# Pooled attention and a ResMLP on one core: rearranging the preamble of batch 0 (constants, bias row, second kpT cast, last heads, lambda alpha1 of the rests)

## The chip, the cores and the metric

The kernel runs on one core of a Trainium2 chip. Times are device microseconds (us) of one execution. Every kernel was run several times, each time beside runs of the kernel before on the same chip; p1 to p3 below are single runs of the change, made for three more profiles.

The engines are called TensorE (PE in the profile; PEld are its weight loads), VectorE (DVE), ScalarE (ACT), GpSimd (POOL), and the queue that issues most loads (SP).

## The reference, cut to what matters

```python
# q, k, v: (8, 8, 576, 64); pool = 8
k_p = k.reshape(B, H, 72, 8, 64).mean(axis=3)
v_p = v.reshape(B, H, 72, 8, 64).mean(axis=3)
attn = softmax(q @ k_p^T / 8)
x = (attn @ v_p)                     # heads joined: (8, 576, 512)
# ResMLP
a1 = alpha1 * x + beta1
u = x + lam * (w_tok @ a1)           # mixes the 576 tokens
a2 = alpha2 * u + beta2
out = u + lam * (relu(a2 @ w_ch1) @ w_ch2)
```

## The kernel before: the parts that matter

The kernel folds lam and alpha1 into `lamal_bc`, keeps `xs = lam*alpha1*x` as the input of the token mixing, and brings in `lam*beta1` as a product of one **bias row** (row 64 of the last chunk of `xs`) with the row sums of w_tok. Each 576-token batch is four chunks of 128 tokens and a rest of 64. Of the helpers that are not shown, `att_F` transposes q, `att_K` spreads the pooled k into `kpT`, `att_S` makes the scores of one head (S) and ScalarE their exponentials (`ET`), `att_Vrem` places the pooled v of the rest, and `keep_warm` issues products that nobody reads, to keep TensorE busy.

```python
def row_of_xs(i, eng):                      # the bias row, 1 x 512
    p0 = 64 - 64 * i
    eng.tensor_tensor(out=xs_pool[i][p0:p0 + 1, 4, :], in0=vecs[p0:p0 + 1, 2],
                      in1=vecs[p0:p0 + 1, 0], op=ALU.mult)

def sum_v(b, u, eng=nc.vector):             # pools 4 heads of v: adds of 512, 256, then 128 columns
    t = st1[b]["v"][u]
    for n in (4, 2):
        eng.tensor_tensor(out=t[:, :, 0:n], in0=t[:, :, 0:n], in1=t[:, :, n:2 * n], op=ALU.add)
    ...

def att_V(b, u, copy):                      # one product spreads pooled v over partitions
    ps_v = gp("ps_v")
    nc.tensor.matmul(out=ps_v[:, 0:128], lhsT=sel_main..., rhs=st1[b]["v"][u]...)
    ...                                     # two casts into vp1
def att_AV(b, h): ...                       # 5 products of a head, then reciprocal and x on VectorE
def att_X(b, h0, h1, eng=nc.vector): ...    # xs = x * lamal, four chunks and the rest
def setup_wtok(tcx, copy): ...              # 5 transposes of w_tok, one evacuation
def setup_rowsum(tcx): ...                  # 5 products with ones, 128 columns each
def mix_T(b, c, eng=nc.vector): ...         # 5 products: one token chunk mixed; then u and u_bf
def mix_uT(key): ...                        # 4 transposes of u, needed by the channel MLP
```

The order in which the preamble of batch 0 issues these (the scheduling is by hand, each engine takes its own in this order):

```python
fill_E()                                    # 12 constants of ET, VectorE
sum_k(0, 0, nc.vector)
cast_rem(0, nc.gpsimd)
cast_q(0, 1, nc.gpsimd.tensor_copy)
row_of_xs(0, nc.vector)
...
load_wtok()                                 # issued by GpSimd
sum_v_rem(0, nc.gpsimd)                     # pools v's rest
for g in range(2):
    load_w1(g)                              # w_ch1, issued by GpSimd
att_S(0, 0); att_S(0, 1)
sum_k(0, 1, nc.vector)                      # the second half of k
att_F(0, 1); att_S(0, 2)
att_K(0, 1, nc.vector.tensor_copy)          # kpT: two casts
att_S(0, 3)
v_00 = st1[0]["v"][0]
sum_v(0, 0)                                 # first half of v, VectorE
att_Vrem(0, nc.scalar.copy)
nc.gpsimd.memset(v_00[:, 0, 0, 0:1], 0.0)   # makes GpSimd wait for VectorE's sum
sum_v(0, 1, nc.gpsimd)                      # second half of v, GpSimd
att_S(0, 4); att_S(0, 5)
att_V(0, 0, nc.vector.tensor_copy)          # "V1" below
att_AV(0, 0) ... att_AV(0, 3)               # with att_S(0, 6), att_S(0, 7), att_X
att_V(0, 1, nc.scalar.copy)                 # "V2" below
setup_wtok(0, nc.scalar.copy)
att_AV(0, 4)
...                                         # w_tok, heads 5 to 7 and row sums in turn
setup_vectors()
keep_warm(2)
mix_T(0, 0)
```

Three moments mark the path in what follows: the **landing of k** (start of VectorE's sum of the second half of k), **V2** (the product that spreads the second half of v, without which heads 4 to 7 cannot start) and **uT** (the first transposes of u).

The softmax here doesn't subtract the row's maximum and nothing guards it: scores larger than these inputs give would overflow.

Of the kernel before, what the change touches and what calls it, by code (L numbers as in the profile page):

```python
# [23 lines left out]
def kernel(  # L24
# [108 lines left out]
    def sum_k(b, u, eng):  # L133

        t = st1[b]["raw"][u][:, 1]
        bf = work.tile([P, 2, 2, D], BF, tag="k_bf", bufs=3, name="k_bf")
        for n in (4, 2):
            eng.tensor_tensor(out=t[:, :, 0:n], in0=t[:, :, 0:n], in1=t[:, :, n:2 * n], op=ALU.add)  # L138
        eng.tensor_tensor(out=bf, in0=t[:, :, 0:1].to_broadcast((P, 2, 2, D)),
                          in1=t[:, :, 1:2].to_broadcast((P, 2, 2, D)), op=ALU.add)  # L140
        st1[b]["k"][u] = bf
# [99 lines left out]
    def fill_E():  # L241
        for t in ET_pool:
            nc.vector.memset(t[:, 0:64], 1.0)
            nc.vector.memset(t[:, 64 + S:], 1.0)
# [25 lines left out]
    def row_of_xs(i, eng):  # L270
# [4 lines that stand above are left out]
# [87 lines left out]
    def att_F(b, u):  # L362



        st = st1[b]
        ps_q = gp("ps_q").bitcast(BF)
        for i in range(8):
            nc.tensor.transpose(  # L369
                out=ps_q[:, 128 * i:128 * i + 128],  # L370
                in_=st["q"][u][:, 2 * i:2 * i + 2].rearrange("p j d -> p (j d)"),
                identity=identity_bf)
        nc.scalar.copy(  # L373
            out=qT_of(b, u)[:, :, 0:256].rearrange("p h (x i) -> p h x i", i=4),
            in_=ps_q.rearrange("p (i a g h) -> p h (a g) i", i=4, a=2, h=4))
# [101 lines left out]
        nc.vector.tensor_tensor(out=x[:, :, dd:dd + D], in0=av[:, :, 0:64],  # L477
                                in1=rec.unsqueeze(2).to_broadcast((P, 5, D)), op=ALU.mult)

    def att_X(b, h0, h1, eng=nc.vector):  # L480

        x, xs = st1[b]["x"], xs_pool[b % 2]
        cols = slice(D * h0, D * h1)
        eng.tensor_tensor(  # L484
            out=xs[:, 0:4, cols], in0=x[:, 0:4, cols],
            in1=lamal_bc[:, cols].unsqueeze(1).to_broadcast((P, 4, D * (h1 - h0))), op=ALU.mult)
        p0 = 64 * (b % 2)
        eng.tensor_tensor(out=xs[p0:p0 + 64, 4, cols], in0=x[p0:p0 + 64, 4, cols],
                          in1=lamal_bc[p0:p0 + 64, cols], op=ALU.mult)
# [111 lines left out]
    nc.scalar.copy(out=lamal_bc, in_=ps_lamal)  # L601
    cast_q(0, 0, nc.vector.tensor_copy)
    att_F(0, 0)
    fill_E()
    sum_k(0, 0, nc.vector)
    cast_rem(0, nc.gpsimd)
    cast_q(0, 1, nc.gpsimd.tensor_copy)
    row_of_xs(0, nc.vector)
    att_Frem(0, (0,), nc.scalar.copy)
    att_K(0, 0, nc.vector.tensor_copy, nc.scalar.copy)  # L610
    att_Frem(0, (1,), nc.vector.tensor_copy)
    load_wtok()
    sum_v_rem(0, nc.gpsimd)
    for g in range(2):
        load_w1(g)
    att_S(0, 0)
# [1 line left out]
    sum_k(0, 1, nc.vector)  # L618
    att_F(0, 1)
    att_S(0, 2)  # L620
    att_K(0, 1, nc.vector.tensor_copy)
    att_S(0, 3)
    v_00 = st1[0]["v"][0]
    sum_v(0, 0)
    att_Vrem(0, nc.scalar.copy)
    nc.gpsimd.memset(v_00[:, 0, 0, 0:1], 0.0)
    sum_v(0, 1, nc.gpsimd)
    att_S(0, 4)
    att_S(0, 5)
    att_V(0, 0, nc.vector.tensor_copy)  # L630
    att_AV(0, 0)
# [7 lines left out]
    att_V(0, 1, nc.scalar.copy)  # L639
    setup_wtok(0, nc.scalar.copy)  # L640
    att_AV(0, 4)
    setup_wtok(1, nc.scalar.copy)
    att_AV(0, 5)
    load_qk(1, 0, nc.vector)
    load_rem(1)
    load_qk(1, 1)
    load_v_rem(1)
    load_v(1, 0)
    load_v(1, 1)
    att_X(0, 4, 6, nc.gpsimd)  # L650
    setup_wtok(2, nc.scalar.copy)
    att_AV(0, 6)
    setup_rowsum(0)
    setup_rowsum(1)
    setup_wtok(3, nc.scalar.copy)
    att_AV(0, 7)
    att_X(0, 6, 8)
    setup_rowsum(2)
    setup_rowsum(3)
    setup_vectors()  # L660
    keep_warm(2)
    mix_T(0, 0)
    mix_T(0, 1)
    mix_T(0, 2, nc.gpsimd)
    mix_uT((0, 0))
# [128 lines left out]
```

## Time and profile before

| | before |
|---|---|
| three runs | 368.33, 368.71, 368.93 us |
| the profiled run | 368.53 us (span 366.7) |
| landing of k, second half | 10.99 us |
| V2 | 19.27 us |
| first mixing of tokens | 25.51 us |
| first transposes of u (uT) | 28.75 us |

A line of the timeline gives start, length, engine, source line, operation, output and inputs by name, the shapes and the count of a merged group. At the end stand the idle time of the engine just before it and what ended that.

VectorE before, its sum of the first half of v in two lines:

```profile
14.96 1.15 DVE L416 TENSOR_TENSOR v_u<-v_u 128x512 f32<-128x512 f32 x2
16.15 0.29 DVE L418 TENSOR_TENSOR v_sum<-v_u 128x128 f16<-128x128 f32 x1
```

The reader is to see three things. GpSimd has issued w_ch1's loads by 15.15 and then stands idle 1.35 us, until VectorE's sum of v has ended at 16.44: VectorE releases it. GpSimd's own sum takes 2.06 us for its first two adds, and V2 starts 2.67 us after that sum began. And V2 has no idle time before it: there TensorE arrived at about the same time as the sum.

In this profile slow matmuls are not to be read from the row of granted clock (the share of TensorE's full clock that the profile lists): it shows full speed in the stretches where the row sum `ps_rs` took 0.62 us as in those where it took 0.39. The durations of like instructions show it.

### The profile page before, as it was taken

The numbers are of one execution on the slowest core, as the hardware profiler recorded it, in microseconds if no ns is written. First come the engines' busy times: TensorE is split into PE (matmuls) and PEld (weight loads), VectorE is DVE, ScalarE is ACT, GpSimd is POOL, SyncE is SP. The second block draws the span as 40 slices with busy tenths as digits, with TensorE's granted clock in tenths as the row PEclk, the third lists the DMA queues.
The fourth block names the chain that finished last, engine by engine and source line by source line (L and its number), as shares of the span: only waits on it lengthen the run. The fifth ranks groups of instructions, "written<-read, shape, count | busy, mean of one in ns | idle before, by whom it ended". The sixth has DMA issues, their size and how long they took to land.

```text
span 366.7 us, 6128 instructions
## 1 busy us (share of the span) xinstructions
PE 352.8 (96%) x2300; PEld 194.5 (53%) x2342; DVE 212.3 (58%) x433; ACT 215.8 (59%) x424; POOL 126.5 (34%) x182
## 2 busy tenths in 40 slices
PE   5799999999999999999999999999999999999995
PEld 2477555455545554555455554555455544544544
DVE  7765534883785368734864388627852687543011
ACT  3865994379628970698259923895279615712710
POOL 8866913072508141452346130905090500000000
PEclk9999999999999999999999999999999999999999
DMA  7999894039103901183108302480110002002002
GB/s 252 268 228 332 226 286 133 22 100 358 53 30 123 323 12 48 57 276 111 59 29 295 124 31 56 139 278 29 50 38 2 29 30 58 2 29 86 2 30 84
DMA packets 19575, 43.27 MB, mean 118 GB/s; under 512 B 2193, under 2 KB 4565, under 8 KB 19546
## 3 DMA queue, kind: packets, MB, share of 16 engines
q1 hardware_dynamic: 17488, 37.89, 30.2%
q0 software_dynamic: 1888, 4.86, 7.0%
q8 instruction: 18, 0.29, 0.3%
q10 hardware_dynamic: 170, 0.14, 0.2%
q14 instruction: 11, 0.09, 0.1%
HBM read 38.30 MB, written 9.44 MB: 130 GB/s over the span
## 4 chain that ended last, share of the span: by engine, by line
PE 87%; ACT 6%; DVE 3%; DMA 2%; issue 1%; SPq 1%; ACTq 0%
PE ps_ch L580 33%; PE ps_h L557 30%; PE ps_tok L510 9%; PE ps_sc L453 4%; ACT Hj L562 3%; PE ps_av L470 2%; PE ps_uT L541 2%; DMA qk_raw<-in_k_dram 2%; PE ps_q L369 1%; PE ps_tok L526 1%; ACT qT L373 1%; PE ps_w L288 1%; SPq L84 1%; PE ps_av L473 1%; PE ps_kp L401 1%
## 5 line engine op out<-in xcount | busy, mean ns | idle before, releaser
L557 PE MATMUL ps_h<-u_fm,w 128*128 128x512 bf16 (+1 forms) x574 | 133.4, 373 | 1.6 <-ACT u_fm L543 0.4
L580 PE MATMUL ps_ch<-w,Hj 128*128 128x512 bf16 x495 | 124.0, 379 | 1.2 <-issue 0.3
L562 ACT ACTIVATE Hj<-ps_h,bias_cols 128x512 bf16<-128x512 f32 x144 | 97.1, 691 | 33.9 <-PE ps_h L557 33.3
L557 PEld LDWEIGHTS <-w 128*128 128x128 bf16 x592 | 63.9, 114 | 48.6 <-issue 0.9
L580 PEld LDWEIGHTS <-Hj 128*128 128x128 bf16 x592 | 55.5, 98 | 49.4 <-issue 0.7
L543 ACT COPY u_fm<-ps_uT 128x512 bf16<-128x512 bf16 x36 | 21.1, 588 | 70.6 <-PE ps_uT L541 70.5
L484 POOL TENSOR_TENSOR xs<-x_tm,lamal_bc 128x512 bf16<-128x512 f32 x24 | 30.6, 1274 | 82.6 <-DVE x_tm L477 82.6
L455 ACT ACTIVATE ET<-ps_sc 128x288 f16<-128x288 f32 (+1 forms) x128 | 51.5, 488 | 11.5 <-PE ps_sc L453 11.1
L408 DVE CAST kpT<-ps_kp 64x288 bf16<-64x288 f32 x31 | 14.1, 455 | 44.0 <-PE ps_kp L404 43.8
L587 DVE TENSOR_TENSOR u_sb<-u_sb,ps_ch 128x512 f32<-128x512 f32 (+1 forms) x37 | 24.9, 673 | 24.9 <-PE ps_ch L580 21.0
L510 PE MATMUL ps_tok<-xs,wtT 128*128 128x512 bf16 (+1 forms) x155 | 38.7, 379 | 0.2
L586 DVE TENSOR_TENSOR ps_ch<-lam_bc,ps_ch 128x512 f32<-128x512 f32 x32 | 22.2, 693 | 25.5 <-PE ps_ch L580 25.4
L475 DVE RECIPROCAL rec<-ps_av 128x5 f32<-128x5 f32 x64 | 12.4, 193 | 36.8 <-PE ps_av L473 36.6
L477 DVE TENSOR_TENSOR x_tm<-ps_av,rec 128x320 f32<-128x320 f32 x64 | 31.5, 492 | 2.8
L138 POOL TENSOR_TENSOR qk_raw<-qk_raw 128x512 f32<-128x512 f32 (+1 forms) x28 | 30.2, 1078 | 1.1
L453 PE MATMUL ps_sc<-qT,kpT 128*128 128x288 bf16 (+1 forms) x128 | 29.4, 306 | 1.0 <-DVE kpT L408 0.8
L512 DVE TENSOR_TENSOR u_sb<-x_tm,ps_tok 128x512 f32<-128x512 f32 x32 | 21.9, 685 | 9.8 <-PE ps_tok L510 9.3
L685 POOL COPY ticks<-ticks 1x1 f32<-1x1 f32 x6 | 1.1, 178 | 70.5 <-DVE ticks L681 70.5
L510 PEld LDWEIGHTS <-wtT 128*128 128x128 bf16 (+1 forms) x160 | 15.0, 98 | 19.1 <-DVE xs L484 2.0
L470 PEld LDWEIGHTS <-ET 72*128 72x128 f16 (+1 forms) x256 | 17.1, 102 | 14.1 <-DVE vp L428 0.6
L513 DVE TENSOR_TENSOR u_bf<-u_sb,al_bc 128x512 bf16<-128x512 f32 x31 | 21.8, 704 | 1.1
L416 DVE TENSOR_TENSOR v_u<-v_u 128x512 f32<-128x512 f32 (+1 forms) x30 | 20.8, 693 | 0.8
(121 smaller groups left out, 338.9 us busy)
## 6 DMA issues: line engine op xcount, KB each, us to landing
qk_raw<-in_q_dram SPq DMA_DIRECT2D x16, 512.0 KB, 6.7
qk_raw<-in_k_dram SPq DMA_DIRECT2D x16, 512.0 KB, 6.5
v_u<-in_v_dram SPq DMA_DIRECT2D x32, 256.0 KB, 6.6
out_dram<-u_sb SPq DMA_DIRECT2D x32, 256.0 KB, 2.2
w<-in_moe_w_ch_dram POOLq DMA_DIRECT2D x2, 1024.0 KB, 14.1
w<-in_moe_w_ch_dram POOLq DMA_DIRECT2D x4, 512.0 KB, 10.8
rem_raw<-in_q_dram SPq DMA_DIRECT2D x8, 128.0 KB, 4.7
rem_raw<-in_k_dram SPq DMA_DIRECT2D x8, 128.0 KB, 4.5
```

The source lines that it names most:

```text
L138: eng.tensor_tensor(out=t[:, :, 0:n], in0=t[:, :, 0:n], in1=t[:, :, n:2 * n], op=ALU.add)
L453: nc.tensor.matmul(out=ps_sc[0:n, 0:288], lhsT=kpT_pool[u][:, j, r, 72 * hh:72 * hh + n], rhs=st["qT"][u][:, h % 4, :])
L455: nc.scalar.activation(out=ET[0:n, 64 + j:64 + S + j:2], in_=ps_sc[0:n, 0:288], func=AF.Exp, bias=0.0, scale=1.0 / 64)
L470: nc.tensor.matmul(out=av[:, c, :], lhsT=ET[:, m0:m0 + 256:2], rhs=vp1)
L477: nc.vector.tensor_tensor(out=x[:, :, dd:dd + D], in0=av[:, :, 0:64], in1=rec.unsqueeze(2).to_broadcast((P, 5, D)), op=ALU.mult)
L484: eng.tensor_tensor(out=xs[:, 0:4, cols], in0=x[:, 0:4, cols], in1=lamal_bc[:, cols].unsqueeze(1).to_broadcast((P, 4, D * (h1 - h0))), op= ...
L510: nc.tensor.matmul(out=ps_tok, lhsT=wtT[0:kk, at, P * c:P * c + P], rhs=xs[0:kk, sc, :], start=(sc == 0), stop=(sc == 4))
L557: nc.tensor.matmul(out=ps_h[:, t0:t1], lhsT=w1_of(cc, j), rhs=u_fm[n][:, cc, t0:t1], start=(cc == 0), stop=(cc == 3))
L562: nc.scalar.activation(out=t, in_=ps_h, func=AF.Relu, bias=bias_cols[:, j:j + 1], scale=1.0)
L580: nc.tensor.matmul(out=ps, lhsT=Hj[n, j][:, 128 * m:128 * m + 128], rhs=w2_of(n, j, cols), start=(j == 0), stop=(j == NJ - 1))
L586: nc.vector.tensor_tensor(out=ps, in0=lam_bc, in1=ps, op=ALU.mult)
L587: nc.vector.tensor_tensor(out=u, in0=u, in1=ps, op=ALU.add)
```

## The change

The intent: VectorE loses work ahead of the first products (the bias row and one cast), TensorE gets the last heads ahead of w_tok's transposes so that their chain on VectorE is done sooner, and the first mixing comes before the last row sum. The parts are lettered as in the prediction.

```diff
-    def att_X(b, h0, h1, eng=nc.vector):
+    def att_X(b, h0, h1, eng=nc.vector, rem=True):
     ...
+        if rem:
+            att_X_rem(b, h0, h1, eng)
+    def att_X_rem(b, h0, h1, eng):          # (e) the 64-row rest on its own
     ...
     att_F(0, 0)
+    sum_k(0, 0, nc.vector)
     fill_E()                                # (a)
-    sum_k(0, 0, nc.vector)
     ...
-    row_of_xs(0, nc.vector)
     ...
     sum_v_rem(0, nc.gpsimd)
+    row_of_xs(0, nc.gpsimd)                 # (b)
     for g in range(2):
         load_w1(g)
     ...
-    att_K(0, 1, nc.vector.tensor_copy)
+    att_K(0, 1, nc.vector.tensor_copy, nc.scalar.copy)      # (c)
     att_S(0, 3)
     v_00 = st1[0]["v"][0]
     sum_v(0, 0)
-    att_Vrem(0, nc.scalar.copy)
     nc.gpsimd.memset(v_00[:, 0, 0, 0:1], 0.0)
     sum_v(0, 1, nc.gpsimd)
     att_S(0, 4)
+    att_Vrem(0, nc.scalar.copy)             # (c)
     ...
     setup_wtok(0, nc.scalar.copy)
     att_AV(0, 4)
+    att_AV(0, 5)                            # (d)
+    att_X(0, 4, 6, nc.gpsimd, False)        # (e)
     setup_wtok(1, nc.scalar.copy)
-    att_AV(0, 5)
     ...                                     # loads of batch 1
-    att_X(0, 4, 6, nc.gpsimd)
+    att_AV(0, 6)
+    att_AV(0, 7)                            # (d)
+    setup_rowsum(0)
     setup_wtok(2, nc.scalar.copy)
-    att_AV(0, 6)
-    setup_rowsum(0)
+    att_X(0, 6, 8, nc.vector, False)
+    att_X_rem(0, 4, 8, nc.vector)           # (e)
     setup_rowsum(1)
     setup_wtok(3, nc.scalar.copy)
-    att_AV(0, 7)
-    att_X(0, 6, 8)
     setup_rowsum(2)
+    keep_warm(2)
+    mix_T(0, 0)                             # (f)
     setup_rowsum(3)
     setup_vectors()
-    keep_warm(2)
-    mix_T(0, 0)
     mix_T(0, 1)
```

## The prediction

> **What bounds the kernel now.** I read the page's busy times first, then the chain of work that ended last, then the same chain in order of time for the first 60 us, and last the timeline of each engine from 9 to 35 us.
>
> ```profile
> PE 352.8 (96%) x2300; PEld 194.5 (53%) x2342; DVE 212.3 (58%) x433; ACT 215.8 (59%) x424; POOL 126.5 (34%) x182
> PE 87%; ACT 6%; DVE 3%; DMA 2%; issue 1%; SPq 1%; ACTq 0%
> ```
>
> The reader is to see that TensorE is on the path for 87% of the span. The matmuls of the eight batches are untouched by this change: the build keeps 4,678 TensorE instructions, and past the first tokens' mixing only line numbers move. All that differs lies before 26 us, in the preamble of batch 0, where TensorE still waits for others. So the gain is bounded by TensorE's lost time there. The chain in order of time shows it (start us, length us, what):
>
> ```profile
> 4.38 6.58 DMA qk_raw<-in_k_dram
> 10.99 0.70 DVE qk_raw L138
> 11.71 1.18 DVE qk_raw L138
> 12.91 0.57 DVE k_bf L139
> 13.99 0.04 DVE kpT L408
> 14.47 0.46 DVE kpT L408
> 14.96 0.70 DVE v_u L416
> 15.69 0.43 DVE v_u L416
> 16.15 0.30 DVE v_sum L418
> 16.50 0.30 PE ps_v L424
> 16.82 0.29 DVE vp L428
> 17.16 0.40 PE ps_av L470 x4
> ...
> 23.76 0.70 ACT wtT L291
> 24.50 0.44 PE ps_rs L300 x5
> 24.94 0.15 PE ps_vec L278
> 25.10 0.32 PE ps_warm L68
> 25.51 3.41 PE ps_tok L510 x15
> ```
>
> Three parts are to be seen. Until 10.96 a transfer of k rules, and nothing done earlier on VectorE can shorten it. From 10.99 to 17.16 VectorE rules: sum of k, two casts of kpT, sum of v, casts of v. From 17.16 TensorE rules, with a last pause near 24 to 25.5 us for w_tok's evacuation and the last heads' products.
>
> A busy table by stretch says the same: TensorE is busy 5.89 of 8.20 us from 9.0 to 17.2, 6.10 of 6.10 from 17.2 to 23.3, 1.77 of 2.20 from 23.3 to 25.5, then 4.99 of 5.00. From 34.4 to 50.7 ScalarE has 15.41 of 16.30 us: it rules there, its work is unchanged, so an earlier start shifts that stage as a whole.
>
> **What the Trainium skill says.**
> "TensorE: Matmul & The Clock Gate", What's actually happening: the array runs at half clock until it has been busy for a free-running window of about 3.4 us. The trace agrees in kind. The timeline shows the same row sum slow at 21.93 and fast at 23.71:
>
> ```profile
> 21.93 0.62 PE L300 MATMUL ps_rs<-wtT,ones_bf 128*128 128x128 bf16 x4
> 23.71 0.39 PE L300 MATMUL ps_rs<-wtT,ones_bf 128*128 128x128 bf16 x4
> ```
>
> Five transposes of w_tok take 0.53 us before about 23.3. The switch thus came about 6 us after the dense stretch began. A microsecond of work saved before it is worth about half of one afterwards, if the switch stays at the same time.
>
> "SBUF — State Buffer", Who interferes with whom: a VectorE instruction with two SBUF inputs contends with a GpSimd instruction that reads SBUF, and the loser blocks wholly. The trace agrees: the 128x256 add of k at 11.71 took 1.167 us beside GpSimd's sums of v's rest (begun at 11.82, 1.36 us for two), where the same shape of v alone took 0.424.
>
> "GPSIMD Engine Reference", 3.1 Elementwise: an add of two tensors is 1.96 times slower there at 2,048 elements. Here the bias row (1x512) took 0.829 us on VectorE and, for the odd batches, 1.261 us on GpSimd, 1.5 times.
>
> **The change part by part.**
>
> (a) ET's constants after the first sum of k. Twelve memsets take 6.00 to 6.92, one per 0.074 us. The sum waits for its transfer, 0.23 us idle, until 7.15. Moved behind, it does not start earlier, since the transfer lands then, and the memsets run from 9.0 to 9.9. The bias row, 9.01 to 9.84, leaves that place. The first kpT cast moves from 9.87 to about 9.94. Worth 0: the next sum of k waits for its transfer until 10.96 anyway.
>
> (b) The bias row goes to GpSimd, ahead of w_ch1's two loads: 1.26 us, from about 13.62 to 14.88. Those loads go out 1.26 us later, at 14.9. The first landed 10.4 us after its issue, that is at 24.0, and is used at 30.23; now 25.3 against some 29.4. Hidden. GpSimd was idle 1.35 us before 16.50, so its own chain (sum of the second half of v) takes no harm.
>
> (c) Half of the second kpT cast on ScalarE. VectorE is free at 14.47 rather than 14.96, 0.49 us on the path. But the sum of v then has two SBUF inputs beside (b)'s row. By the add at 11.71 (it effectively began at 12.88 - 0.42 = 12.46, before GpSimd was done) I let it start at 14.73. That leaves 0.23 us. V's rest, moved after S of head 4, is evacuated by ScalarE at 16.45 to 17.2, its first half at 16.82. V's casts end at 16.85. The first product begins at about 16.93 against 17.16: 0.23 us. The second half of v comes from GpSimd only 0.07 to 0.1 us earlier (it cannot start before w_ch1's loads are issued, 16.4), so that **about 0.1 us** is left at head 4.
>
> (d) The heads' products ahead of w_tok. From head 4 at 19.92 (20.02 before): heads 4 and 5 to 20.45, transposes 1 to 20.98, heads 6 and 7 to 21.55, row sum 0 to 22.1, transposes 2 to 22.6, row sum 1 to 23.15, transposes 3 to 23.5, row sum 2 to 23.9, two warming matmuls to 24.35. On VectorE four heads take 0.65 us each from 20.44, so the last is done at 23.1 instead of 24.63. Its multiplication by lambda alpha1 (0.69 us) may be held by GpSimd's own for heads 4 and 5 until 23.3 or 23.5, and ends at 24.0 to 24.3.
>
> (e) The rests apart: GpSimd loses one 64x128 product, 0.45 us; VectorE's 64x128 (0.28) becomes 64x256 (some 0.4), and is needed only by the fifth matmul of a mixing. Hidden: 24.4 to 24.7 against 24.4 + 4 x 0.22 = 25.3.
>
> (f) The first mixing starts at 24.4 rather than 25.51, 1.1 us earlier. But row sum 3 and the beta2 transpose (0.3 + 0.15) now come after it. I also count that the waits at 24.15 (0.35) and 25.4 (0.1) are gone: 0.45 us, with 0.1 from (c) and 0.2 to 0.3 from passing the slow-clock work sooner. Both ways the sum is **0.65 to 0.85 us** at the end of the third mixing (28.91 before, about 28.1 after). I take 0.8.
>
> Behind it, q of batch 1 is issued after head 5, about 0.2 us earlier, and lands 8.7 us later, at about 30.6; GpSimd would want it at 30.65. No wait, or one which its slack hides. ScalarE's full stage begins at 33.6 rather than 34.41 and all shifts.
>
> 368.71 - 0.8 = 367.9.
>
> **The rivals.**
> 1. VectorE and GpSimd collide more than I allow: the sum of v waits for the whole row (14.9) and the last lambda alpha1 product for GpSimd's whole 1.27 us. For it: the 1.167 us above. Then (c) gives nothing and the mixing starts at 24.6: 0.5 us gained, 368.2.
> 2. The clock switches at another time. It is free-running, so an earlier window would make the 3.4 us before 23.3 faster, up to 0.8 us more, until ScalarE's four evacuations of w_tok (0.77 each in a run) bind: 367.1. A later window puts the mixings on the slow clock (0.43 instead of 0.22 us per 512 columns, by the 106 ns per 128 seen before): a loss of about 1 us eats the gain, 368.8. The three runs of before spread over 0.6 us, so I give each about one in eight.
> 3. ScalarE becomes the bound: it gets a cast (0.39) and its V rest later. Against it: it idles 0.87 us before 18.23, and S of heads 6 and 7 waits for the buffer that V's rest frees at 17.2, which is in time.
> 4. The gain is hidden behind a load, w_ch1 or batch 1's. The busy table's DMA share is over 1.0 until 34 us. Against: 4 us of slack for w_ch1, and no wait of GpSimd for a load is seen. It would leave 368.5.
>
> **Range and chances.** The central sum gives 367.9; I put 367.8, as small waits on the path tend to vanish together. Rivals 1 and 4 reach 368.2 to 368.5, the clock 367.1 to 368.8, and medians move by 0.3. Range 366.9 to 368.6. Two per cent is 7.4 us: more than TensorE's whole idle time in the preamble from 9 us on (2.3 + 0.4), so faster has 0.01. Slower by as much would need a stall that nothing here shows: 0.01.
>
> **What would show it.** (a) and (b): the second k sum still at 10.99, no wait for w_ch1 before the bias columns. (c): the sum of v begins near 14.47 but its first add lasts longer than 0.69 us; first product near 16.93. (d) to (f): last head done near 23.1, first mixing near 24.4, first transpose of u near 28.1, first full Hj near 33.6, and the same lead at 60 us and at the end. The prediction is wrong if the lead at 28 us is not the lead at the end (a stage between eats it), if the row sums change speed elsewhere than near 23.3, or if GpSimd waits for batch 1's q.

## More of the kernel before

TensorE before: V1, V2 and the first transposes of u:

```profile
16.50 0.29 PE L424 MATMUL ps_v<-v_sum,sel_main 128*128 128x128 f16 x1 [0.58 <-DVE v_sum L418]
...
19.27 0.30 PE L424 MATMUL ps_v<-v_sum,sel_main 128*128 128x128 f16 x1
...
28.75 0.39 PE L541 MATMUL ps_uT<-identity_bf,u_bf 128*128 128x128 bf16 x4
```

GpSimd before: the sum of v's rest, the issue of w_ch1's loads, the memset that waits for VectorE, the sum of the second half of v:

```profile
11.82 1.36 POOL L434 TENSOR_TENSOR rem_v_raw<-rem_v_raw 64x256 f32<-64x256 f32 x2
...
13.60 1.55 POOL L324 DMA_DIRECT2D w<-in_moe_w_ch_dram  x2
16.50 0.10 POOL L626 MEMSET v_u<- 128x1 f32 x1 [1.35 <-DVE v_sum L418]
16.60 2.06 POOL L416 TENSOR_TENSOR v_u<-v_u 128x512 f32<-128x512 f32 x2
```

## The result

| | before | after |
|---|---|---|
| six runs each | 368.10 to 368.99, median 368.52 | 367.45 to 369.56, median 368.94 |
| the profiled run | 368.53 | 369.56 |
| landing of k, second half | 10.99 | 10.69 |
| V2 | 19.27 | 20.09 |
| first mixing | 25.51 | 25.83 |
| uT | 28.75 | 29.86 |

The ratio is 1.0006, with a 95% interval of 0.9983 to 1.0029: no difference shown. A ratio here is the mean time of one kernel's fast runs over that of the other's of the same rounds, so it is not quite the ratio of the medians quoted. The predicted 367.8 was not reached; the median lies outside the range.

TensorE after, the lines that answer to those of before, and the third row sum:

```profile
15.88 0.29 PE L424 MATMUL ps_v<-v_sum,sel_main 128*128 128x128 f16 x1 [0.21 <-DVE v_sum L418]
...
20.09 0.26 PE L424 MATMUL ps_v<-v_sum,sel_main 128*128 128x128 f16 x1 [1.25 <-POOL v_sum L418]
...
24.44 0.63 PE L300 MATMUL ps_rs<-wtT,ones_bf 128*128 128x128 bf16 x4
...
29.86 0.39 PE L547 MATMUL ps_uT<-identity_bf,u_bf 128*128 128x128 bf16 x4
```

GpSimd after:

```profile
11.93 1.47 POOL L434 TENSOR_TENSOR rem_v_raw<-rem_v_raw 64x256 f32<-64x256 f32 x2 [0.61 <-DMA rem_v_raw<-in_v_dram]
13.48 0.77 POOL L435 TENSOR_TENSOR vrem<-rem_v_raw 64x64 f16<-64x64 f32 x1
14.33 1.34 POOL L273 TENSOR_TENSOR xs<-vecs 1x512 bf16<-1x512 f32 x1
15.62 1.58 POOL L324 DMA_DIRECT2D w<-in_moe_w_ch_dram  x2
...
17.42 2.08 POOL L416 TENSOR_TENSOR v_u<-v_u 128x512 f32<-128x512 f32 x2
```

VectorE after, its first two adds of the second half of k and the sum of v:

```profile
10.69 1.15 DVE L138 TENSOR_TENSOR qk_raw<-qk_raw 128x512 f32<-128x512 f32 x2 [0.49 <-DMA qk_raw<-in_k_dram]
...
13.40 1.14 DVE L416 TENSOR_TENSOR v_u<-v_u 128x512 f32<-128x512 f32 x2
14.57 1.25 DVE L418 TENSOR_TENSOR v_sum<-v_u 128x128 f16<-128x128 f32 x1
```

k landed 0.30 us earlier than in the profile of before, and V1 came 0.62 us earlier, the first head too (16.54 against 17.16). Then the lead was lost. TensorE stood idle for 1.25 us in front of V2, which waited for GpSimd's sum of v. GpSimd began that sum at 17.42 rather than 16.60: it had waited 0.61 us for its rest of v (whose sum began at 11.93, against 11.82 before), its last add of the rest took 0.77 instead of 0.38, beside VectorE's adds of v, the bias row started at 14.33 and not at the predicted 13.62, and the loads of w_ch1 were issued behind it. VectorE's last add of v took 1.25 instead of 0.29, beside the row. And the row sum at 24.44 still took 0.63 us; before, the row sum at 23.71 already took 0.39.

From the first transposes of u to the end, both kernels take the same: 368.53 - 28.75 = 339.78 and 369.56 - 29.86 = 339.70 us. So the loss arises ahead of uT, and whatever lead or lag stands there reaches the end.

### The profile page after: what moved, and what is told of

The parts are those of the page before. It is cut to its first block, busy times and chain, and to the rows that moved or that the text cites. A ratio compares the mean times of both kernels' runs of the same rounds, so it can differ in the third digit from the quotient of the medians.

```text
span 367.8 us, 6170 instructions
## 1 busy us (share of the span) xinstructions
PE 355.9 (97%) x2342; PEld 195.2 (53%) x2342; DVE 210.8 (57%) x431; ACT 216.2 (59%) x425; POOL 127.5 (35%) x182
## 4 chain that ended last, share of the span: by engine, by line
PE 89%; ACT 4%; POOL 3%; DVE 2%; issue 1%; POOLq 0%; ACTq 0%
PE ps_ch L586 33%; PE ps_h L563 31%; PE ps_tok L516 10%; PE ps_sc L453 4%; PE ps_uT L547 2%; ACT Hj L568 2%; PE ps_av L470 2%; PE ps_q L369 2%; PE ps_tok L532 1%; PE ps_rs L300 1%; PE ps_w L288 1%; POOL v_u L416 1%; PE ps_av L473 1%; ACT qT L373 0%; POOL b2row L214 0%
## 5 line engine op out<-in xcount | busy, mean ns | idle before, releaser
L586 PE MATMUL ps_ch<-w,Hj 128*128 128x512 bf16 x512 | 127.2, 379 | 0.0
L516 PE MATMUL ps_tok<-xs,wtT 128*128 128x512 bf16 (+1 forms) x160 | 39.7, 381 | 0.0
L416 DVE TENSOR_TENSOR v_u<-v_u 128x512 f32<-128x512 f32 (+1 forms) x30 | 20.5, 683 | 0.8
```

The costliest lines, as they stand in the source:

```text
L516: nc.tensor.matmul(out=ps_tok, lhsT=wtT[0:kk, at, P * c:P * c + P], rhs=xs[0:kk, sc, :], start=(sc == 0), stop=(sc == 4))
L586: nc.tensor.matmul(out=ps, lhsT=Hj[n, j][:, 128 * m:128 * m + 128], rhs=w2_of(n, j, cols), start=(j == 0), stop=(j == NJ - 1))
```

## The experiments

**How they are read.** From this follows a sum that every profile is checked against: landing of k, plus the time from there to V2, plus the time from V2 to uT, plus about 339.8 us (340.4 in e3 and 340.5 in r14). The table has it for all profiled runs. A profiled run is one run of its kernel and not always a typical one: it was the slowest in the change's first profile, e2, e13 and r14, and the fastest in e8, e9 and e11. "Row" is where the bias row is computed. "Rest" is the idle time of GpSimd in front of the sum of v's rest, ended by that transfer. "Ahead" is how long before VectorE's sum of v the row started (minus: after it).

| kernel | row | k | rest | ahead | k to V2 | V2 to uT | profiled us |
|---|---|---|---|---|---|---|---|
| before | VectorE | 10.99 | none | | 8.28 | 9.48 | 368.53 |
| after | GpSimd | 10.69 | 0.61 | -0.93 | 9.40 | 9.77 | 369.56 |
| r5_after_again | GpSimd | 10.44 | none | 0.64 | 8.26 | 8.87 | 367.36 |
| p1_change | GpSimd | 10.82 | 0.43 | 0.64 | 8.25 | 9.41 | 368.19 |
| p2_change | GpSimd | 11.52 | 1.15 | 0.11 | 9.11 | 9.37 | 369.80 |
| p3_change | GpSimd | 11.52 | none | 0.64 | 8.07 | 8.89 | 368.17 |
| e2_row_only | GpSimd | 11.24 | 1.12 | -0.08 | 9.31 | 9.73 | 370.06 |
| e4_fill_wait | GpSimd | 11.18 | 0.89 | 0.12 | 9.47 | 8.57 | 369.01 |
| e12_change_filled | GpSimd | 11.35 | 0.46 | 0.28 | 9.28 | 8.88 | 369.23 |
| e8_vrem_queue | GpSimd | 10.90 | none | 0.64 | 8.54 | 8.90 | 368.13 |
| e3_w1_later | GpSimd | 11.33 | 0.31 | 0.64 | 7.94 | 10.32 | 369.96 |
| e5_row_behind_w1 | GpSimd | 11.06 | 0.60 | -0.86 | 8.52 | 8.88 | 368.24 |
| e6_memset_queue | VectorE | 10.45 | none | | 10.02 | 9.57 | 369.74 |
| e11_queue_filled | VectorE | 10.80 | none | | 9.94 | 8.88 | 369.42 |
| e1_row_vector | VectorE | 10.78 | none | | 7.91 | 8.67 | 367.23 |
| e7_row_vector_vrem | VectorE | 11.10 | 0.90 | | 7.71 | 8.85 | 367.52 |
| e9_rowsum_first | VectorE | 11.17 | 1.04 | | 7.80 | 8.60 | 367.26 |
| e13_row_vector_filled | VectorE | 11.81 | 1.41 | | 7.68 | 8.89 | 368.19 |
| r14_row_vector_again | VectorE | 11.54 | 0.71 | | 7.96 | 8.92 | 368.94 |
| e10_both | VectorE | 11.03 | none | | 8.29 | 9.21 | 368.44 |

Empty cells do not apply. The timed results, with the median of the kernel before on the same chip (it had 6 runs in the first row, 11 or so in the others):

| kernel | runs, us | median | before | ratio, 95% interval |
|---|---|---|---|---|
| change (first time) | 367.45, 368.39, 368.42, 369.45, 369.49, 369.56 | 368.94 | 368.52 | 1.0006 [0.9983, 1.0029] |
| r5_after_again | 367.31, 367.36, 367.36, 369.29, 369.61, 369.64 | 368.32 | 367.87 | 1.0015 [0.9991, 1.0040] |
| e1_row_vector | 367.23 to 367.57 (5) | 367.28 | 367.76 | 0.9986 [0.9974, 0.9998] |
| r14_row_vector_again | 367.22 to 368.94 (6) | 367.67 | 367.79 | 1.0003 [0.9987, 1.0019] |
| e7_row_vector_vrem | 367.04 to 367.79 (5) | 367.52 | 367.87 | 0.9989 [0.9976, 1.0002] |
| e2_row_only | 367.74 to 370.06 (6) | 368.42 | 367.76 | 1.0021 [1.0003, 1.0038] |
| e3_w1_later | 369.91 to 370.18 (5) | 369.96 | 367.76 | 1.0059 [1.0047, 1.0071] |
| e4_fill_wait | 368.64 to 369.64 (5) | 369.01 | 367.76 | 1.0032 [1.0018, 1.0047] |
| e5_row_behind_w1 | 368.20 to 369.04 (6) | 368.24 | 367.87 | 1.0015 [1.0002, 1.0027] |
| e6_memset_queue | 369.42 to 371.61 (6) | 370.18 | 367.87 | 1.0069 [1.0050, 1.0089] |
| e8_vrem_queue | 368.13 to 369.88 (6) | 368.61 | 367.77 | 1.0027 [1.0013, 1.0042] |
| e9_rowsum_first | 367.26 to 368.46 (5) | 367.64 | 367.77 | 1.0000 [0.9988, 1.0013] |
| e10_both | 368.15 to 368.60 (5) | 368.27 | 367.77 | 1.0015 [1.0002, 1.0028] |
| e11_queue_filled | 369.42 to 371.21 (6) | 370.32 | 367.77 | 1.0070 [1.0054, 1.0085] |
| e12_change_filled | 367.72 to 369.26 (6) | 368.88 | 367.78 | 1.0022 [1.0007, 1.0037] |
| e13_row_vector_filled | 367.26 to 368.19 (5) | 367.59 | 367.79 | 0.9993 [0.9981, 1.0006] |

All gave correct results. All moves are under 1%, and only the intervals tell more.

**The theories.** The queue (Q): the row, 1.26 us in GpSimd's queue, puts off w_ch1's loads and the sum of v behind them. The port (P): the row and VectorE's adds of v hold each other up. The clock (C): the switch of the matmuls to their faster rate comes late, which costs whatever is slow until then.

### e1: the row on VectorE, all else as in the change

```diff
-    row_of_xs(0, nc.gpsimd)                  # behind sum_v_rem
 ...
     sum_k(0, 1, nc.vector)
+    row_of_xs(0, nc.vector)                  # in VectorE's wait for kpT's products
     att_F(0, 1)
```

> The changed kernel with one part undone: the bias row is back on VectorE, in its wait of 0.73 us between the second sum of k and the kpT cast. Theory Q (GpSimd's queue): the row held w_ch1's loads and with them the sum of the second half of v, so the product that places this half (20.09 us in the changed kernel, 19.27 before) now starts near 18.2 to 18.8, TensorE's wait of 1.25 us ahead of it is gone, the add that ends the first half of v lasts 0.29 us instead of 1.25, and the first transposes of u come at 28.0 to 28.6 instead of 29.86; time 367.3 to 368.0. Theory C (clock alone: the switch fell a window later by chance): the queue moves but the first transposes of u stay within 0.3 us of 29.86 whenever the switch is late, and the time keeps the spread of 367.5 to 369.5.

VectorE, the row and the sum of v:

```profile
12.97 0.69 DVE L273 TENSOR_TENSOR xs<-vecs 1x512 bf16<-1x512 f32 x1
...
14.17 1.15 DVE L416 TENSOR_TENSOR v_u<-v_u 128x512 f32<-128x512 f32 x2
15.36 0.29 DVE L418 TENSOR_TENSOR v_sum<-v_u 128x128 f16<-128x128 f32 x1
```

TensorE, V2 and uT:

```profile
18.69 0.30 PE L424 MATMUL ps_v<-v_sum,sel_main 128*128 128x128 f16 x1
...
27.36 0.39 PE L547 MATMUL ps_uT<-identity_bf,u_bf 128*128 128x128 bf16 x4
```

The row takes 0.69 us, all but some 0.2 of it in a wait (the products for the next kpT cast had ended at 13.41, the cast began at 13.69), and the sum of v its undisturbed 1.15 and 0.29. GpSimd's loads were issued by 14.62, ahead of the end of VectorE's sum at 15.65, so VectorE again releases GpSimd, as in the kernel before. The path from k to V2 is 7.91 us, against 8.28 before and 9.40 in the changed kernel's first profile, and the five runs lie within 0.34 us. So with (b) undone the rest of the change does no harm. Whether it gains over before is less sure: the second time (r14 below) the interval has both signs.

### e2: the row alone, on the kernel before

```diff
-    row_of_xs(0, nc.vector)
 ...
     sum_v_rem(0, nc.gpsimd)
+    row_of_xs(0, nc.gpsimd)
     for g in range(2):
```

> The kernel before with one part of the change alone: the bias row on GpSimd ahead of w_ch1's loads. Theory Q: w_ch1's loads go out at 14.9 to 15.6 instead of 13.60, the product that places the second half of v starts at 19.8 to 20.3 instead of 19.27, and the time is 0.3 to 1.2 us over the kernel before. Theory C: GpSimd had 1.35 us to spare, so that product stays within 0.2 us of 19.27 and the time within 0.2 us.

```profile
14.42 1.73 POOL L273 TENSOR_TENSOR xs<-vecs 1x512 bf16<-1x512 f32 x1
...
20.55 0.27 PE L424 MATMUL ps_v<-v_sum,sel_main 128*128 128x128 f16 x1 [0.77 <-POOL v_sum L418]
```

Slower than before by 0.21%, with the interval above 1. The profiled run took 370.06 us, the slowest of the six (the others took 367.74 to 368.86), and also had all four row sums slow: the path from k to V2 was 9.31 us, v's rest was waited for 1.12 us, the row took 1.73 us from 14.42, and w_ch1's loads and V2 were later than the expectation had them (16.10 and 20.55). It loses by (b) alone, without any other part of the change. Queue and port both act here; the next runs part them.

### e3: the loads of w_ch1 behind GpSimd's sum of v

```diff
-    for g in range(2):
-        load_w1(g)
     ...
     sum_v(0, 1, nc.gpsimd)
+    for g in range(2):
+        load_w1(g)
```

> The changed kernel with w_ch1's two loads issued behind the sum of the second half of v; the row stays on GpSimd. Theory Q says that the harm is the order in the queue: the sum starts near 16.0 instead of 17.42, its product at 18.5 to 18.9 instead of 20.09, and the add that ends the first half of v still lasts over 1 us, for the row still holds the shared port. The first w_ch1 load lands near 28.8, just before its use at 30; time 367.5 to 368.3. A rival theory P (the port: the 1.25 us add on VectorE is what costs) expects no gain: the first product of a head stays at 16.5 and the time within 0.3 us of the changed kernel's.

A miss. The path to V2 did shorten, to 7.94 us, which is what the queue predicts, though only in part by it: this profile is of the group in which the row is well ahead (see p1 to p3), whose paths are 8.07 to 8.54 us with the loads in their place. But the loads now stood in front of GpSimd's products with lambda alpha1, and the first mixing waited for these:

```profile
25.81 1.24 PE L516 MATMUL ps_tok<-xs,wtT 128*128 128x512 bf16 x5 [1.36 <-POOL xs L484]
```

The 1.36 us there made V2 to uT 10.32 us, and every run was at about 370. The wait was moved, not removed.

### e4: TensorE's wait ahead of V2 filled

```diff
+    keep_warm_ch(3)                          # three products of 512 columns, into a free buffer
     att_V(0, 1, nc.scalar.copy)
```

> The changed kernel with three idle matmuls of 128x512 put where TensorE waits 1.25 us for the second half of v, so that it hardly stops between 16.5 us and the mixings. The product for this half stays at 20.1. Theory C+ (the wait also put off the clock's switch by one window): the row sums change speed near 23.3 instead of 26.7, the first transposes of u come at 28.6 to 29.3 instead of 29.86, the time falls by 0.5 to 1.2 us. If the clock does not depend on that wait: no change beyond 0.2 us, or a loss of up to 0.2 us by the idle matmuls.

V2 to uT fell to 8.57 us with no slow row sum (the last slow products, transposes of w_tok, began at 21.86), which fits with a pause of TensorE there costing part of a late clock; it is one profile. But the median of 369.01 is no better than the change's: V2 itself was late (9.47 us after k, of which the filling products took some 0.3, as V2 came 2.96 us after GpSimd's sum began rather than 2.65).

### r5: the change again, on another chip

> The changed kernel once more, for its spread beside the next three on one chip. In its first six runs it took 367.45 to 369.56. If the row's collisions and the clock's switch depend on when loads land, the runs spread again over more than 1 us, where the row on VectorE spread over 0.34; the median lies 0.5 to 2 us over that kernel's. The end stays 339.7 to 339.9 us behind the first transposes of u, as in the profiles so far.

Three runs at 367.3, three at 369.3 to 369.6: the change has two groups of times, 2 us apart. This profile fell in the fast group. GpSimd:

```profile
11.14 1.36 POOL L434 TENSOR_TENSOR rem_v_raw<-rem_v_raw 64x256 f32<-64x256 f32 x2
...
13.03 1.26 POOL L273 TENSOR_TENSOR xs<-vecs 1x512 bf16<-1x512 f32 x1
14.24 1.57 POOL L324 DMA_DIRECT2D w<-in_moe_w_ch_dram  x2
```

VectorE, its adds of k and of v:

```profile
10.44 1.75 DVE L138 TENSOR_TENSOR qk_raw<-qk_raw 128x512 f32<-128x512 f32 x2 [0.29 <-DMA qk_raw<-in_k_dram]
...
13.67 1.63 DVE L416 TENSOR_TENSOR v_u<-v_u 128x512 f32<-128x512 f32 x2
```

TensorE, V2 and uT:

```profile
18.70 0.27 PE L424 MATMUL ps_v<-v_sum,sel_main 128*128 128x128 f16 x1
...
27.57 0.39 PE L547 MATMUL ps_uT<-identity_bf,u_bf 128*128 128x128 bf16 x4
```

Here v's rest was there without a wait, the row started at 13.03, w_ch1's loads were issued by 15.81, only 0.18 us after VectorE's sum had ended, and TensorE had no pause before V2. The prediction reckoned with this course. Note that k landed at 10.44: counted from there, V2 is no earlier than before (8.26 against 8.28). What it gains comes from V2 to uT, 8.87 against 9.48.

### e5: the row behind w_ch1's loads (port without queue)

```diff
     for g in range(2):
         load_w1(g)
+    row_of_xs(0, nc.gpsimd)
```

> The row stays on GpSimd but behind w_ch1's loads, in the queue's own wait: the port without the queue. Expected: w_ch1's loads at 13.1 to 13.9; the row at 14.6 to 15.9 beside VectorE's sum of v, which is stretched from 1.44 us in all to 2.0 to 2.5; first head's product near 17.0 to 17.3 instead of 16.54; the product of the second half of v near 19.0 to 19.4 (18.69 with the row on VectorE, 20.09 in the change), no wait of TensorE over 0.4 us before it. Time 0.2 to 0.6 us over the row on VectorE. If the port is what costs in the change, it should be as slow as the change.

The loads went out undisturbed, by 15.02. But the row ran from 15.08 beside VectorE's last add of v:

```profile
14.22 1.13 DVE L416 TENSOR_TENSOR v_u<-v_u 128x512 f32<-128x512 f32 x2
15.39 1.24 DVE L418 TENSOR_TENSOR v_sum<-v_u 128x128 f16<-128x128 f32 x1
```

1.24 us instead of 0.29 for that add. VectorE's sum ended at 16.63, GpSimd's own sum waited for it and began at 16.92, and the path to V2 was 8.52 us, 0.61 over e1's. The median was 368.24, against 367.5 for e7. So the port costs by itself, and here the row could not have cost by delaying the loads.

### e6: GpSimd's queue filled without the port

Six memsets of 64 x 512, which read nothing, in place of the row; the row is on VectorE.

```diff
     sum_v_rem(0, nc.gpsimd)
+    for _ in range(6):
+        nc.gpsimd.memset(xs_pool[1][0:64, 4, :], 0.0)
     for g in range(2):
```

> The row on VectorE, and in its old place on GpSimd six memsets (some 2.5 us) that read nothing: the queue without the port. Expected: VectorE's sum of v at 1.44 us as undisturbed; w_ch1's loads at 15.5 to 15.8; the second half's sum at 17.2 to 17.5, its product at 19.9 to 20.2, with a wait of TensorE of 1.1 to 1.4 us as in the change. If the queue and its wait are what costs: time as the change's, 1 to 2 us over the row on VectorE, and the switch of the clock mostly after 25 us. If the port is what costs: time within 0.4 us of the row on VectorE.

GpSimd, then VectorE, then V2 on TensorE:

```profile
12.84 3.39 POOL L620 MEMSET xs<- 64x512 bf16 x6
16.18 1.56 POOL L324 DMA_DIRECT2D w<-in_moe_w_ch_dram  x2
```

```profile
13.95 1.15 DVE L416 TENSOR_TENSOR v_u<-v_u 128x512 f32<-128x512 f32 x2
15.13 0.29 DVE L418 TENSOR_TENSOR v_sum<-v_u 128x128 f16<-128x128 f32 x1
```

```profile
20.47 0.27 PE L424 MATMUL ps_v<-v_sum,sel_main 128*128 128x128 f16 x1 [1.42 <-POOL v_sum L418]
```

VectorE's adds took 1.15 and 0.29, as if GpSimd stood still: no port. Yet GpSimd's sum began at 17.77, TensorE waited 1.42 us before V2, and the median was 370.18. The queue alone is enough for the loss, given a delay of its size (3.39 us of memsets here, more than the row).

### e7: e1 with V's rest in its old place

```diff
     sum_v(0, 0)
+    att_Vrem(0, nc.scalar.copy)
     ...
     att_S(0, 4)
-    att_Vrem(0, nc.scalar.copy)
```

> The row on VectorE and, besides, v's rest evacuated ahead of S of head 4 as in the kernel before. In the run with the row on VectorE the first head's product waited 0.60 us for that evacuation (16.54). Expected: it starts at 16.2 to 16.3, while the second half of v still comes at 18.6 to 18.7, so TensorE waits 0.2 to 0.3 us there and the mixing moves by 0 to 0.1: time within 0.2 us of 367.28 scaled to this chip. If the early part counts fully: 0.25 us faster.

367.52, beside 367.28 for e1 on another chip. The place of V's rest in (c) makes no difference that these runs show. The profile also has a wait of 0.90 us for v's rest, and still a path to V2 of 7.71 us: with the row on VectorE a late rest does no harm.

### p1, p2, p3: the change, three more profiles

> The changed kernel, one profile more. Whatever group the run falls into: the time is 339.7 to 339.9 us over the start of the first transposes of u. If the queue makes the group, a run near 369.5 has the product of v's second half at 19.8 or later with a wait over 0.8 us, one near 367.4 has it at 18.5 to 18.9. If the clock makes it, runs near 369.5 have slow row sums after 24.5 us whatever the queue did.

> The changed kernel, one profile more, with the same two readings as the one before it: where v's second half is placed, and up to when the row sums are slow.

> The changed kernel, one profile more, with the same two readings: where v's second half is placed, and up to when the row sums are slow.

They gave 368.19, 369.80 and 368.17 us. p2 is of the slow kind. GpSimd and VectorE in p2:

```profile
12.53 1.32 POOL L434 TENSOR_TENSOR rem_v_raw<-rem_v_raw 64x256 f32<-64x256 f32 x2 [1.15 <-DMA rem_v_raw<-in_v_dram]
...
14.31 1.92 POOL L273 TENSOR_TENSOR xs<-vecs 1x512 bf16<-1x512 f32 x1
16.18 1.57 POOL L324 DMA_DIRECT2D w<-in_moe_w_ch_dram  x2
```

```profile
14.42 2.09 DVE L416 TENSOR_TENSOR v_u<-v_u 128x512 f32<-128x512 f32 x2
```

v's rest was waited for 1.15 us, the row started at 14.31, 0.11 us before VectorE's sum of v, and both were held: 1.92 us instead of 1.26, and 2.09 instead of 1.15. The loads of w_ch1 ended 0.91 us after VectorE's sum.

p1 has no late sum of v but the late clock. TensorE in p1, two heads on either side of 17.75 us:

```profile
16.98 0.30 PE L470 MATMUL ps_av<-vp,ET 128*128 128x66 f16 x4
...
18.21 0.43 PE L470 MATMUL ps_av<-vp,ET 128*128 128x66 f16 x4
```

The same products take 0.30 us at 16.98 and 0.43 at 18.21. Here the granted clock shows it too: it falls to 0.50 at 17.75 and is full again from 24.6. In the 3.4 us before it fell TensorE was busy for 2.33 us, and no pause was over 0.62 us. So the faster rate can be lost again after short pauses alone. In e1, e7 and e9 it was lost in the same way, from about 17 to 20.5 us.

Over the ten profiles with the row ahead of w_ch1's loads on GpSimd the table divides cleanly. Where the row started 0.64 us ahead of VectorE's sum of v (r5, p1, p3, e3, e8), VectorE's pair of adds waited once (1.63 instead of 1.15) and the path to V2 was 7.94 to 8.54. Where it started 0.28 ahead or later (after, p2, e2, e4, e12), row and adds held each other longer, and the path was 9.11 to 9.47. In the first group v's rest was waited for 0.43 us at most, in the second at least 0.46.

One step earlier the profiles divide in the same way. In the first group GpSimd's sum of v's rest began at most 0.84 us after k landed, and VectorE's first two adds of k, which then run beside it, took 1.56 to 2.02 us; so VectorE came late to v, and the row was ahead of it. In the second group that sum began at least 0.89 us after k landed, and the adds of k took 1.15. All twenty profiles divide so (1.56 us or more up to 0.84, 1.15 from 0.87 on). What counts is thus when GpSimd gets to v's rest, be it for the transfer or for its own work before; this is read from the profiles, and no run varied it alone.

The changed kernel's fifteen runs (both sets of six and p1 to p3) divide as well: eight at 367.31 to 368.42, seven at 369.29 to 369.80, none between.

### e12: the change with the clock kept fast

```diff
+    keep_warm_ch(1)                          # in each of TensorE's waits from 9 to 17 us, five in all
 ...
+    keep_warm_ch(2)
     att_V(0, 1, nc.scalar.copy)
```

> The changed kernel with seven idle matmuls of 128x512 in TensorE's pauses: five between 9 and 17 us, two before v's second half. If the clock's late switch makes the slow group, that group is gone: the switch comes before 20 us, times lie within 0.8 us of one another, at 367.3 to 368.3, and what is left between them is the queue's 0 to 1 us. If the queue alone makes it: times still from 367.4 to 369.5. If the idle matmuls delay the first heads by more than they save: all times over 368.5.

TensorE, V2 and the first row sum:

```profile
20.63 0.22 PE L424 MATMUL ps_v<-v_sum,sel_main 128*128 128x128 f16 x1 [0.96 <-POOL v_sum L418]
...
22.22 0.38 PE L300 MATMUL ps_rs<-wtT,ones_bf 128*128 128x128 bf16 x4
```

No slow row sum is left, and V2 to uT is 8.88. But the runs still spread from 367.72 to 369.26, median 368.88, and this profile has V2 after a wait of 0.96 us, for GpSimd. So the clock does not make the two groups; the late sum of v does (by this profile and p1's, which has the late clock in the good group; the other runs of e12 have no profile). The clock adds 0.5 to 0.9 us where it comes late on top (V2 to uT of 9.37 to 9.77 against 8.87 to 8.89).

### e11: e6 with TensorE's wait filled

```diff
     (as e6)
+    keep_warm_ch(3)
     att_V(0, 1, nc.scalar.copy)
```

> The kernel with six memsets in GpSimd's queue (370.18 us, TensorE's wait 1.42 us, clock switch after 25.3) with three idle matmuls in that wait: the wait without the pause. Theory C+ (a pause of TensorE puts the switch off): second half of v still placed at 20.3 to 20.7, row sums fast from some time before 24.2, first transposes of u at 28.9 to 29.4 instead of 30.04: time 0.6 to 1.2 us under 370.18. If the pause is harmless to the clock: 370.0 to 370.3.

In the profile the filling did what it should: V2 to uT fell from 9.57 to 8.88. The median of 370.32 (on another chip) did not fall below e6's 370.18, though, so the expected gain of the clock was missed in the times. The first mixing now waited 0.94 us for VectorE's last product with lambda alpha1. When V2 is this late the heads' chain on VectorE is the next limit.

### e8: v's rest loaded first, from another queue

```diff
-    load_v_rem(0)                            # behind both halves of q and k
 ...
+    load_v_rem(0, nc.scalar)                 # issued by ScalarE, at the start
     nc.scalar.activation(out=start[:, 1:2], ...)
```

> The changed kernel with one difference: the load of v's rest is issued from ScalarE's queue near 2.7 us rather than as the sixth load of SyncE's at 5.03, so that it lands early. Theory L (the landing of v's rest chooses between the change's two outcomes: with it at hand GpSimd reached the row at 13.03 and the run took 367.36; 0.61 us late, the row began at 14.33 and the run took 369.56): GpSimd never waits for this load, the row begins near 12.9 to 13.1 and the second half of v is placed at 18.5 to 18.9 in every run, so the time is 367.2 to 367.9 with a spread under 0.6 us. Theory C (the clock alone chooses): the queue as said, but the times stay in two groups, near 367.4 and 369.5.

A miss. In the profile the rest is there without a wait and the row is 0.64 us ahead of VectorE's sum, as hoped. But the path to V2 is 8.54 us, and the times spread as widely as the change's, 368.13 to 369.88. Only the fastest of the six runs was profiled, so what made the slow ones isn't shown. The early load does disturb others: GpSimd now waited 0.48 us for the rest of k (0.37 in e10), and SyncE issued the second half of k at 4.71 instead of 4.39. GpSimd therefore began its sum of v's rest 0.84 us after k landed, the latest start of the first group.

### e9 and e10: the last row sum before the first mixing; and with e8's load as well

```diff
     (e9: as e1, and)
-    keep_warm(2)
-    mix_T(0, 0)
+    keep_warm(1)
     setup_rowsum(3)
     setup_vectors()
+    mix_T(0, 0)
```

> The row on VectorE, and the fourth row sum and the beta2 transpose again ahead of the first mixing, with one idle matmul instead of two. In the run with the row on VectorE, TensorE waited 0.38 us for xs there. Expected: that work (0.45 us) fits into the wait, the first transposes of u come 0.2 to 0.4 us sooner (27.0 to 27.2 if all else is as in that run): 0.2 to 0.4 us faster. If the fourth evacuation of w_tok ends too late (23.27 there), the mixing starts later and nothing is gained.

> The last one, with v's rest loaded from ScalarE's queue besides: if late landing costs nothing once the row is off GpSimd, the same time within 0.2 us; if it still costs, a smaller spread and 0.2 us less. A candidate to beat both kernels: 366.6 to 367.4 where the kernel before takes 367.8.

e9 filled the wait before the first mixing (V2 to uT 8.60, the least of all with V2 in time), and its median of 367.64 is no better than before's 367.77. e10, with the early load of v's rest, is slower by 0.15%. Both expectations of a gain were missed, and neither is a version to keep.

### r14 and e13: e1 again, and e1 with the clock kept fast

> The row on VectorE, once more. If v's second half alone sets the end of the preamble, it is placed at 18.5 to 19.0, the first transposes of u start 8.6 to 9.0 us later where the clock switched before 23, and the time is 367.1 to 367.7, 0.3 to 0.6 us under the kernel before; the spread stays under 0.8 us.

> The same with five idle matmuls in TensorE's pauses before 17 us. In the changed kernel filled so, the first transposes of u came 8.88 us after v's second half, as in every run whose clock switched in time. So here: switch before 19 us, no gain over the row on VectorE where that switched in time (8.67 to 8.9 us), 0.5 us at most where it did not. Median within 0.3 us of the run above; a loss of over 0.3 us would say that the idle matmuls are in the way.

On another chip e1's kernel gave a median of 367.67 beside 367.79, and a spread of 1.7 us, from 367.22 to 368.94. So e1's spread of 0.34 was partly luck, and its advantage over the kernel before is not shown. Of the eleven runs of this kernel, eight have a mean granted clock of 0.995 and took 367.22 to 367.98; the other three (0.998 to 1.000), among them the profiled run of r14, took 367.57, 368.25 and 368.94. In e1's profile the 0.995 is the stretch at 0.50 from 16.8 to 20.2 us, after an early switch; r14's profile shows the rarer course, with its first row sum still slow at 21.89. But the slow group is gone: of the 31 runs with the row on VectorE and a free queue (e1, r14, e7, e9, e10, e13) none took over 368.94 us, and seven of the change's fifteen did. What both profiles confirm is the path from k to V2: 7.96 and 7.68 us. Filling the waits (e13) took away every slow row sum and changed nothing in the times that the intervals show. r14's profile has its 368.94 from a k landing at 11.54 and, as in one other profile (e3), from time lost after uT (340.52 us to the end, 0.7 more than usual). The trace shows where: GpSimd waited 1.85 us for the rest of q of batch 1, its pooled k came late, and TensorE stood idle for 0.56 us before spreading it, at 38.65. In e3 GpSimd waited 0.34 and 1.49 us for the rests of q and k there, TensorE 0.40.

## Why the prediction was wrong, point by point

**The step that failed is (b).** "GpSimd was idle 1.35 us before 16.50, so its own chain (sum of the second half of v) takes no harm." The row takes 1.26 us of these 1.35, and (c) was to move the end of the idle time, VectorE's sum, forward at the same time. The margin was thus about 0.1 us even on paper, as (c) itself says with its 16.4. And it rested on a row that starts at 13.62 and takes 1.26 us. In the changed kernel's five profiles the row started at 13.03, 13.39, 13.93, 14.31 and 14.33, and took up to 1.92: v's rest, which is summed before it, was waited for up to 1.15 us, and in the two late cases VectorE's adds of v were already there or close behind, and row and adds held each other. The profile of before showed no such wait, and one profile cannot show how much a landing moves.

What took its place: GpSimd's sum starts behind the later of two things, VectorE's sum and the issue of w_ch1's loads, and V2 came 2.64 to 2.70 us after that start wherever TensorE was not the later one.

| | VectorE's sum ended | w_ch1's loads issued by | GpSimd's sum began | V2 |
|---|---|---|---|---|
| before | 16.44 | 15.15 | 16.60 | 19.27 |
| after | 15.82 | 17.20 | 17.42 | 20.09 |
| r5 | 15.63 | 15.81 | 16.04 | 18.70 |
| p2 | 16.84 | 17.75 | 17.98 | 20.63 |
| e1 | 15.65 | 14.62 | 15.81 | 18.69 |
| e6 (queue only) | 15.42 | 17.74 | 17.77 | 20.47 |
| e5 (port only) | 16.63 | 15.02 | 16.92 | 19.58 |

In the good runs the loads are 0.2 us behind VectorE's sum, in the bad ones 0.9 to 1.4. e6 shows that the queue suffices, e5 that the port costs too, e1 that without either the path is short. Counted from the landing of k, GpSimd's sum began at 5.61 us before, at 5.43 to 5.60 in r5, p1 and p3 (no harm, but no gain), and at 6.46 and 6.73 in p2 and the first profile. And none of the 51 timed runs of the kernel before (367.00 to 368.99 us) lies in the change's slow group.

**The sum, term by term.** Over the changed kernel's five profiles, k landed on average at 11.00 (10.99 in the profile of before), k to V2 took 8.62 us and V2 to uT 9.26. Against before that is +0.34 and -0.22; predicted were about -0.1 and -0.55 to -0.75. The first error is the step above. The second is the late clock, in three of the five.

**What was right.** (a) costs and gives nothing: the second sum of k still starts when its transfer lands. The later loads of w_ch1 are hidden from their users: nothing waits for them ahead of the bias columns. (c) brings the first head forward: it came 5.73 to 6.04 us after the landing of k in the five profiles, against 6.17 before (predicted 5.94). The order of (d) to (f) may be worth its 0.6 us: V2 to uT was 8.87 in r5 against 9.48 before, and in both the products became fast about 4 us after V2. But it is one pair of profiles, and with a later clock no gain is seen: 9.73 in e2, in the old order, beside 9.37 to 9.77. The lead or lag at uT is the lead or lag at the end, as said. The eight runs of the good group have a median of 367.81 us, the predicted figure; the prediction took that course for the only one. That the figure fits is luck: it was reckoned from a kernel before at 368.71, whose median on the four later chips was 367.8 without any change.

**The rivals.** Rival 1, the collision of VectorE and GpSimd, came true in both halves: VectorE's sum of v was held for 0.48 to 0.96 us, and its last product with lambda alpha1 took 1.26 to 1.28 us in all five profiles (0.69 before). But its cost was put at 368.2, since the queue behind the row was not in it. Rival 2, the clock, was real, but its loss of about 1 us was given one chance in eight: three of five profiles had a late clock, at 0.5 to 0.9 us. ScalarE (rival 3) was last to release the first head in r5 and in six profiles with the row on VectorE (e1, e9, e10, e11, e13, r14), where TensorE waited 0.39 to 0.60 us for it, against mostly 0.38 for VectorE elsewhere: a few tenths at most. A load on the path (rival 4) cost after k's landing only by way of GpSimd's queue, in v's rest and, in r14 and e3, in batch 1's rests of q and k; in the changed kernel's own profiles GpSimd waited there 0.89 us at most (r5), and the slack hid it, as the prediction allowed. Two readings of the prediction don't hold as they stand, and nothing hangs on them: from 34.4 to 50.7 us TensorE was busier (15.85 of 16.30 us) than ScalarE, which "rules there"; and the count of 4,678 TensorE instructions stands in no view of the record.

**What stays open.** The kernel before was profiled once, in a run of 368.53; on four later chips its median was 367.8, so the profile may have caught a slow course of it (it has slow row sums until 23). How its other runs divide is not known. That the good group of the change is no faster than before's usual runs fits with this, but is only argued. What chooses the group within a kernel is not settled either: the profiles go with how soon after k GpSimd gets to v's rest, but that was not set by hand, and e8's slow runs have no profile. And no version here is shown beyond doubt to beat the kernel before: e1's kernel is the best candidate, with one interval below 1 and one across it.

## What to carry to other kernels

Idle time of an engine is no free room when its end is released by another engine that the same change makes faster, and when what is put there stands ahead of the work that the path needs: compare the later of the two releases, with the spread of the landings, not the mean of one profile. Look for DMA issues in such a queue, because here what stood in front of them was passed on to the sum behind them. And profile a change of this size several times, before and after, since two groups of runs 2 us apart hide a gain of 0.8.

## What the Trainium skill lacked or had wrong

- "TensorE: Matmul & The Clock Gate", What's actually happening, says that the clock drops back after an idle window of about 3.4 us. In p1 the granted clock fell to 0.50 at 17.75, and the same products took 0.30 us at 16.98 and 0.43 at 18.21, although TensorE had been busy for 2.33 of the 3.4 us before and no idle time was over 0.62. For a loss by such short pauses the page gives no length. It also calls the count of slow matmuls variable between runs, which the runs confirm, and the moment of the switch uncertain by half a microsecond. Here the last slow products of the preamble began anywhere from 20.01 (e1) to 26.00 us (e2), with first heads at 16.54 and 17.48, and a late clock cost 0.5 to 0.9 us of a run.
- "SBUF — State Buffer", Who interferes with whom: confirmed in both ways (GpSimd's 1 x 512 product held VectorE's adds, memsets on GpSimd did not). That the order of issue decides is borne out only in part by the starts in the profiles: with the row 0.64 us ahead VectorE's first add was held (1.17 us instead of 0.67 in p1), but with it 0.11 to 0.28 us ahead (p2, e4, e12) that add took 0.67 us, the row was held (1.92 to 2.08 us instead of 1.26), and the second add paid. The page has no size for it: VectorE's sum lost 0.48 us when the row started 0.64 us ahead, and 0.94 to 0.96 when it started within 0.3 us of the adds or behind them.
- No page says how much the landing of the same load moves between runs of one kernel: the second half of k was used from 10.44 to 11.52 us in the changed kernel's five profiles, and v's rest was waited for between 0 and 1.15 us. That spread is part of what undid this prediction.
- "GPSIMD Engine Reference", 3.1 Elementwise, compares an operation on two tensors at 2,048 elements only; the 1 x 512 product here took 1.26 us on GpSimd and 0.69 to 0.83 on VectorE, 1.5 to 1.8 times.
